# Batches 1 to 7 of x: transposed by DMA from the bf16 copy in SBUF, where TensorE transposed them through PSUM

## The chip, the cores and the metric

The kernel runs on one core of one Trainium2 chip. The metric is the device time of one execution in microseconds; the median of the runs is compared. Durations inside the kernel come from one profiled execution of it.

## The reference

For 8 batches, 8 heads, 512 tokens of x, 32 state rows and a head width of 64, tokens read the state and the state reads the tokens; both results are joined and go through a gated feed-forward layer.

```python
scores = scale * x @ state.T            # per batch and head, softmax over the 32 state rows
xread  = softmax(scores) @ state
scores2 = scale * state @ x.T           # softmax over the 512 tokens
sread  = softmax(scores2) @ x
a = concat([xread, sread])              # (8 * 544, 512): heads side by side
gate = 1 / (1 + exp(-(a @ w_gate)))     # 512 -> 1536
val  = a @ w_val
out  = (gate * val) @ w_out             # 1536 -> 512, float32
```

## The kernel before

**The work of a batch.** Matmul operands are bf16. The token scores need x with the head width on the partitions, so every batch of x is transposed: `at_xT` takes the bf16 copy `xb` (tokens on the partitions, 4 chunks c of 128 tokens, 512 columns each). In two halves, i = 0 and 1, PE makes eight 128x128 transposes into a PSUM tile `xTp` (line 107), and DVE copies the tile to `xT` in SBUF (line 108). `at_S` then multiplies `xT` with the state: half i covers the chunks 2i and 2i+1, with eight matmuls of 64 columns (line 117), and ACT takes the exponential (line 119). `at_norm`, `at_aT` and `at_sr` normalise, transpose the attention weights (`aT`) and compute the state's read.

**The feed-forward part.** `sw_tile` multiplies the state of a batch with the gate and value weights once (`SW`, line 177), so that `gv` makes gate and value rows straight from `aT` and `SW` (line 192, ACT tanh at 199, DVE product at 200). `out_mm` multiplies the result with the output weights (line 209). ACT evicts each finished tile `res` (line 213) and SP stores it (line 216).

**The order.** It is written by hand: a loop over b (the batch in its feed-forward part) and, inside, over f from 0 to 11. One step f holds a third of an output tile of batch b-1, a 128-row piece of gate and value of batch b, one `sw_tile` of batch nb = b+1, and one stage of the attention of batch nb. Each engine works through its instructions in this order. Batch 0's attention runs ahead of the loop. In the steps that matter here:

```python
if f == 0:
    at_xT(nb, 0)
    if b > 0 and nb + 1 < B:
        load_x(nb + 1)
elif f == 1:
    at_xT(nb, 1)
elif f == 2:
    at_S(nb, 0)
elif f == 3:
    at_S(nb, 1)
```

**The queues.** Nearly all transfers are issued by SP, in program order: loads of x (`load_x`, 1 MB), of the weights (`load_w`, `load_wo`), and the stores of `out_mm`, the last of which in an iteration comes at f = 11. GpSimd (POOL) casts each x to bf16 (`cast_x`, line 89) at f = 11 of the iteration before the one that transposes it, behind the casts of `Eb` (line 124); batch 1 is cast ahead of the loop.

Of the kernel before, what the change touches and what calls it, by code (L numbers as in the profile page):

```python
# [9 lines left out]
BF = mybir.dt.bfloat16  # L10
# [6 lines left out]
def kernel(  # L17
# [13 lines left out]
    nc = tc.nc  # L31
# [12 lines left out]
    ap_ = ctx.enter_context(tc.tile_pool(name="ap", bufs=2))  # L44
# [14 lines left out]
    xfs, wfs, xbs, xTs = {}, {}, {}, {}  # L59
# [3 lines left out]
    def load_x(b):  # L63
        xf = stg.tile((128, H, 4, D), FP, name="xf", tag="stg")
        v = x[b].rearrange("h (p c) d -> p h c d", c=4)
        if b == 0:
            for i in range(2):
                nc.sync.dma_start(xf[:, 4 * i:4 * i + 4], v[:, 4 * i:4 * i + 4])
        else:
            nc.sync.dma_start(xf, v)  # L70
        xfs[b] = xf

    def load_w(src, key, q):
        wf = stg.tile((128, 4, 512), FP, name="wf", tag="stg")
        nc.sync.dma_start(wf, src.rearrange("(k p) n -> p k n", p=128)[:, :, q * 512:(q + 1) * 512])
        wfs[key, q] = wf

    def load_wo(q):
        wf = stg.tile((128, 4, 512), FP, name="wof", tag="stg")
        nc.sync.dma_start(wf, moe_w_out.rearrange("(k p) n -> p k n", p=128)[:, 4 * q:4 * q + 4])  # L80
        wfs["o", q] = wf
# [13 lines left out]
    def cast_wo(q):  # L95
        for i in range(4):
            nc.gpsimd.tensor_copy(wo[:, 4 * q + i], wfs["o", q][:, i])


    def at_xT(b, i):  # L100
        if i == 0:
            xTs[b] = ap_.tile((128, 4, 512), BF, name="xT")
        ps = p_at.tile((128, 2, 4, 128), BF, name="xTp", tag="at")
        for jj in range(2):
            for c in range(4):
                j = 2 * i + jj
                nc.tensor.transpose(ps[:, jj, c], xbs[b][:, c, 2 * j:2 * j + 2].rearrange("p h d -> p (h d)"), ident)  # L107
        nc.vector.tensor_copy(xTs[b][:, 2 * i:2 * i + 2], ps.rearrange("p j c t -> p j (c t)"))  # L108

    def at_S(b, i):  # L110
        if i == 0:
            E1s[b] = ap_.tile((128, 4, H * Ns), FP, name="E1")
        ps = p_at.tile((128, 2, H * Ns), FP, name="Sp", tag="at")
        for cc in range(2):
            c = 2 * i + cc
            for j in range(4):
                nc.tensor.matmul(ps[:, cc, j * 64:(j + 1) * 64], xTs[b][:, j, c * 128:(c + 1) * 128],  # L117
                                 sTz[:, b, j, 0:64], start=True, stop=True)
        nc.scalar.activation(E1s[b][:, 2 * i:2 * i + 2], ps, AF.Exp, scale=scale)  # L119

    def at_Eb(b):
        Ebs[b] = ap_.tile((128, 4, H * Ns), BF, name="Eb")
        for c in range(4):
            nc.gpsimd.tensor_copy(Ebs[b][:, c], E1s[b][:, c])  # L124

    def at_norm(b, i):
        if i == 0:
            abs_[b] = ap_.tile((128, 4, H * Ns), BF, name="ab")
        E = E1s[b][:, 2 * i:2 * i + 2].rearrange("p c (h n) -> p (c h) n", n=Ns)
        rs = ap_.tile((128, 16), FP, name="rs")  # L130
        nc.vector.tensor_reduce(rs, E, AX.X, ALU.add)  # L131
        ri = ap_.tile((128, 16), FP, name="ri")
        nc.vector.reciprocal(ri, rs)  # L133
        nc.vector.tensor_tensor(abs_[b][:, 2 * i:2 * i + 2].rearrange("p c (h n) -> p (c h) n", n=Ns), E,  # L134
                                ri.unsqueeze(2).to_broadcast((128, 16, Ns)), ALU.mult)

    def at_aT(b):
        ps = p_at.tile((128, 2, 4, 128), BF, name="aTp", tag="at")
        for g in range(2):
            for c in range(4):  # L140
                nc.tensor.transpose(ps[:, g, c], abs_[b][:, c, g * 128:(g + 1) * 128], ident)  # L141
        aTs[b] = ap_.tile((128, 2, 512), BF, name="aT")
        nc.vector.tensor_copy(aTs[b], ps.rearrange("p g c t -> p g (c t)"))
# [23 lines left out]
    def sw_tile(b, t):  # L167
        if t == 0:
            SWs[b] = fp.tile((128, 2, 2, dff), BF, name="SW", bufs=2)
        q, w, g = t // 4, (t // 2) % 2, t % 2  # L170
        ps = p_sw.tile((128, 512), FP, name="swp")
        W = wg if w == 0 else wv
        for jj in range(2):
            j = 2 * g + jj
            flat = sTz[:, b].rearrange("p j e -> p (j e)")
            lo = j * 128 - 64 * jj
            nc.tensor.matmul(ps, flat[:, lo:lo + 128], W[:, j, q * 512:(q + 1) * 512],  # L177
                             start=(jj == 0), stop=(jj == 1))
        nc.scalar.activation(SWs[b][:, g, w, q * 512:(q + 1) * 512], ps, AF.Copy)  # L179


    def gv(b, f):
        n = 512 if b < B else B * Ns
        if f == 0:
            glus[b] = fp.tile((128, NF, n), BF, name="glu", bufs=2, padded_shape=(128, NF, 512))
        fs = slice(f * 128, (f + 1) * 128)
        pss = []
        for w in range(2):
            ps = p_gv.tile((128, 512), FP, name="gvp", tag="gv")[:, :n]
            if b < B:  # L190
                for g in range(2):
                    nc.tensor.matmul(ps, SWs[b][:, g, w, fs], aTs[b][:, g], start=(g == 0), stop=(g == 1))  # L192
            else:
                for j in range(4):
                    nc.tensor.matmul(ps, (wg if w == 0 else wv)[:, j, fs], XS[:, j], start=(j == 0), stop=(j == 3))  # L195
            pss.append(ps)
        th = fp.tile((128, 512), FP, name="th")[:, :n]

        nc.scalar.activation(th, pss[0], AF.Tanh, scale=0.5)  # L199
        nc.vector.scalar_tensor_tensor(glus[b][:, f], th, 1.0, pss[1], ALU.add, ALU.mult)  # L200
# [3 lines left out]
    def out_mm(b, k):  # L204
        c, f0 = k // 3, (k % 3) * 4
        if f0 == 0:
            ops[b, c] = p_out.tile((128, 512), FP, name="outp")
        for f in range(f0, f0 + 4):
            nc.tensor.matmul(ops[b, c], glus[b][:, f, c * 128:(c + 1) * 128], wo[:, f],  # L209
                             start=(f == 0), stop=(f == NF - 1))  # L210
        if f0 == 8:
            res = fp.tile((128, 512), FP, name="res")
            nc.scalar.activation(res, ops[b, c], AF.Copy, scale=0.5)  # L213
            if b < B:
                rows = out[b * SC:b * SC + S].rearrange("(p c) n -> c p n", c=4)
                nc.sync.dma_start(rows[c], res)
            else:
                for i in range(4):
                    r0 = (4 * c + i) * SC + S
                    nc.sync.dma_start(out[r0:r0 + Ns], res[i * Ns:(i + 1) * Ns])  # L220
# [46 lines left out]
    for b in range(B + 1):  # L267
        for f in range(NF):
            nb = b + 1 if b + 1 < B else None
            if b == 0:  # L270
                if f % 4 == 0:
                    for t in range(f, f + 4):
                        sw_tile(0, t)
                if f == 1:
                    load_w(moe_w_gate, "g", 2)
                    load_w(moe_w_val, "v", 2)
                if f in (4, 5, 6):
                    load_wo(f - 4)
                if f in (8, 9, 10):
                    cast_wo(f - 8)  # L280
            if b > 0:
                out_mm(b - 1, f)
            gv(b, f)
            if nb is not None:
                sw_tile(nb, f)
                if f == 0:
                    at_xT(nb, 0)
                    if b > 0 and nb + 1 < B:
                        load_x(nb + 1)
                elif f == 1:  # L290
                    at_xT(nb, 1)
                elif f == 2:
                    at_S(nb, 0)
                elif f == 3:
                    at_S(nb, 1)
                elif f == 4:
                    at_norm(nb, 0)
                    at_Eb(nb)
                elif f == 5:
                    at_norm(nb, 1)  # L300
                elif f == 6:
                    at_aT(nb)
                elif f == 8:
                    at_sr(nb)
                if b == 0 and f == 9:
                    load_x(2)
                if nb + 1 < B and f == 11:
                    cast_x(nb + 1, nc.gpsimd, range(4))
            if b == 0 and f in (3, 7):
                cast_w(f // 4 + 1)  # L310
# [32 lines left out]
```

## Time and profile before

| | us |
|---|---|
| median of 3 runs | 294.54 (294.14 to 294.59) |
| the profiled execution | 292.45 |
| its span | 290.7 |
| PE matmuls busy, of the span | 254.0 (87%) |
| VectorE (DVE) busy | 131.7 (45%) |
| ScalarE (ACT) busy | 152.8 (53%) |
| GpSimd (POOL) busy | 37.4 (13%) |

The span runs from the first to the last recorded instruction; the profiled execution's time is 1.75 us longer than its span. PE's busy share is an average over a slow start, a long middle in which the loop over f runs, and the end. TensorE's granted clock is full in every slice of the page. The rows name engines as PE (matmul), PEld (weight load, which overlaps PE), DVE, ACT, POOL and SPq (SP's queue of DMA issues).

### The profile page before, as it was taken

The page shows a single profiled execution, that of the slowest core. Times are in us where ns is not written, and L with a number is a line of the kernel's source. Part 1 is how long each engine was busy: PE and PEld are TensorE (multiplying, and loading weights), DVE is VectorE, ACT ScalarE, POOL GpSimd, SP SyncE. Part 2 cuts the span into 40 slices and gives each one's busy share as a digit, 9 for nine tenths or more (in the row PEclk, how much of TensorE's full clock was granted, in tenths as well). Part 3 has the DMA queues.
Part 4 walks back from the last instruction along what each step waited for, and adds up shares of the span by engine and source line. Part 5 has one row for each costly group of instructions (what it writes and reads, how often), then busy time and mean ns, then how long its engine had stood idle before and what let it go on. Part 6 is the DMA issues. An engine that isn't in the chain of part 4 may idle for free.

```text
span 290.7 us, 4172 instructions
## 1 busy us (share of the span) xinstructions
PE 254.0 (87%) x1600; PEld 130.8 (45%) x1600; DVE 131.7 (45%) x216; ACT 152.8 (53%) x264; POOL 37.4 (13%) x78
## 2 busy tenths in 40 slices
PE   0044688599999999999999999999999999999993
PEld 0034243245454545454545454545454544456651
DVE  3026364654554455445544554455445543342210
ACT  0333378675755575557555655565566554432330
POOL 0006016800500050005000500050002000000000
PEclk9999999999999999999999999999999999999999
DMA  7977706900110611061105101511101001011102
GB/s 229 338 241 270 293 2 227 341 12 6 53 41 29 177 54 38 28 178 53 39 26 182 48 37 33 183 39 36 38 36 39 36 36 39 36 72 38 72 37 72
DMA packets 20276, 27.53 MB, mean 95 GB/s; under 512 B 3104, under 2 KB 11296, under 8 KB 20256
## 3 DMA queue, kind: packets, MB, share of 16 engines
q1 hardware_dynamic: 18080, 26.74, 27.1%
q10 hardware_dynamic: 2176, 0.52, 0.9%
q8 instruction: 12, 0.20, 0.3%
q14 instruction: 8, 0.07, 0.1%
HBM read 18.35 MB, written 8.91 MB: 94 GB/s over the span
## 4 chain that ended last, share of the span: by engine, by line
PE 77%; DVE 10%; DMA 5%; ACT 4%; issue 1%; ACTq 0%; DVEq 0%
PE outp L209 28%; PE gvp L192 25%; PE swp L177 12%; DMA sf<-in_state_dram 5%; PE gvp L195 4%; PE xTp L107 3%; DVE glu L200 3%; DVE rs L131 3%; DVE ab L134 2%; PE aTp L141 2%; PE srp L157 1%; PE srp L152 1%; ACT wv L93 1%; PE Sp L117 1%; DVE ri L133 1%
## 5 line engine op out<-in xcount | busy, mean ns | idle before, releaser
L200 DVE SCALAR_TENSOR_TENSOR glu<-th,gvp 128x512 bf16<-128x512 f32 (+1 forms) x108 | 70.9, 657 | 124.4 <-ACT th L199 107.4
L209 PE MATMUL outp<-wo,glu 128*128 128x512 bf16 x408 | 104.1, 379 | 0.7 <-ACT res L213 0.7
L192 PE MATMUL gvp<-aT,SW 128*128 128x512 bf16 x384 | 99.7, 382 | 0.1
L199 ACT ACTIVATE th<-gvp 128x512 f32<-128x512 f32 (+1 forms) x108 | 61.7, 572 | 65.5 <-PE gvp L192 55.1
L179 ACT ACTIVATE SW<-swp 128x512 bf16<-128x512 f32 x96 | 56.9, 597 | 30.3 <-PE swp L177 30.3
L192 PEld LDWEIGHTS <-SW 128*128 128x128 bf16 x384 | 37.5, 98 | 45.6 <-ACT SW L179 1.6
L209 PEld LDWEIGHTS <-glu 128*128 128x128 bf16 x408 | 37.9, 98 | 38.0 <-issue 1.0
L124 POOL CAST Eb<-E 128x256 bf16<-128x256 f32 x32 | 13.0, 435 | 179.8 <-ACT E L119 179.8
L177 PE MATMUL swp<-wg,sTz 128*128 128x512 bf16 x96 | 28.9, 389 | 6.4 <-DVE wg L92 6.4
L177 PEld LDWEIGHTS <-sTz 128*128 128x128 bf16 x192 | 19.0, 100 | 31.2 <-issue 6.9
L213 ACT ACTIVATE res<-outp 128x512 f32<-128x512 f32 x34 | 20.3, 597 | 21.0 <-PE outp L209 21.0
L177 PE MATMUL swp<-wv,sTz 128*128 128x512 bf16 x96 | 29.0, 389 | 0.7 <-ACT SW L179 0.7
L108 DVE COPY xT<-xTp 128x1024 bf16<-128x1024 bf16 x16 | 11.1, 691 | 13.8 <-PE xTp L107 13.7
L89 POOL CAST xb<-xf 128x512 bf16<-128x512 f32 x28 | 16.8, 642 | 0.8 <-DMA xf<-in_x_dram 0.8
L246 PE MATMUL stp<-ident,sb 128*128 128x128 bf16 x8 | 1.2, 306 | 16.4 <-ACT sb L243 16.4
L134 DVE TENSOR_TENSOR ab<-E,ri 128x512 bf16<-128x512 f32 x16 | 12.6, 785 | 0.6
L141 PE MATMUL aTp<-ident,ab 128*128 128x128 bf16 x64 | 6.6, 231 | 5.9 <-DVE ab L134 5.2
L107 PE MATMUL xTp<-ident,xb 128*128 128x128 bf16 x128 | 10.6, 230 | 1.1 <-DVE xb L89 1.1
L131 DVE TENSOR_REDUCE rs<-E 128x16 f32<-128x512 f32 x16 | 10.8, 676 | 1.2 <-ACT E L119 1.2
L107 PEld LDWEIGHTS <-xb 128*128 128x128 bf16 x128 | 9.1, 103 | 4.7 <-DVE xb L89 1.4
L119 ACT ACTIVATE E<-Sp 128x512 f32<-128x512 f32 x16 | 9.4, 592 | 3.1 <-PE Sp L117 3.1
L160 DVE RECIPROCAL r<-srp 128x128 f32<-128x128 f32 x8 | 7.7, 957 | 4.0 <-PE srp L157 4.0
(31 smaller groups left out, 102.6 us busy)
## 6 DMA issues: line engine op xcount, KB each, us to landing
out_dram<-res SPq DMA_DIRECT2D x32, 256.0 KB, 2.2
xf<-in_x_dram SPq DMA_DIRECT2D x7, 1024.0 KB, 7.2
wf<-in_moe_w_gate_dram SPq DMA_DIRECT2D x3, 1024.0 KB, 8.3
wf<-in_moe_w_val_dram SPq DMA_DIRECT2D x3, 1024.0 KB, 5.3
wof<-in_moe_w_out_dram SPq DMA_DIRECT2D x3, 1024.0 KB, 5.0
xf<-in_x_dram SPq DMA_DIRECT2D x2, 512.0 KB, 4.8
sf<-in_state_dram ACTq DMA_DIRECT2D x8, 64.0 KB, 8.0
out_dram<-res SPq DMA_DIRECT2D x8, 64.0 KB, 1.7
```

The lines of the kernel that those rows point to most:

```text
L89: eng.tensor_copy(xb.rearrange("p c h d -> p h c d")[:, 2 * i:2 * i + 2], xf[:, 2 * i:2 * i + 2])
L107: nc.tensor.transpose(ps[:, jj, c], xbs[b][:, c, 2 * j:2 * j + 2].rearrange("p h d -> p (h d)"), ident)
L124: nc.gpsimd.tensor_copy(Ebs[b][:, c], E1s[b][:, c])
L131: nc.vector.tensor_reduce(rs, E, AX.X, ALU.add)
L134: nc.vector.tensor_tensor(abs_[b][:, 2 * i:2 * i + 2].rearrange("p c (h n) -> p (c h) n", n=Ns), E, ri.unsqueeze(2).to_broadcast((128, 16, ...
L177: nc.tensor.matmul(ps, flat[:, lo:lo + 128], W[:, j, q * 512:(q + 1) * 512], start=(jj == 0), stop=(jj == 1))
L179: nc.scalar.activation(SWs[b][:, g, w, q * 512:(q + 1) * 512], ps, AF.Copy)
L192: nc.tensor.matmul(ps, SWs[b][:, g, w, fs], aTs[b][:, g], start=(g == 0), stop=(g == 1))
L199: nc.scalar.activation(th, pss[0], AF.Tanh, scale=0.5)
L200: nc.vector.scalar_tensor_tensor(glus[b][:, f], th, 1.0, pss[1], ALU.add, ALU.mult)
L209: nc.tensor.matmul(ops[b, c], glus[b][:, f, c * 128:(c + 1) * 128], wo[:, f], start=(f == 0), stop=(f == NF - 1))
L213: nc.scalar.activation(res, ops[b, c], AF.Copy, scale=0.5)
```

## The change

The two calls of `at_xT` inside the loop go. In their place, at f = 0, SP issues four DMA transposes per batch, one per chunk of 128 tokens: each reads 128 x 512 bf16 (128 KB) of `xb` and writes 128 x 4 x 128 of `xT`. Batch 0 is still transposed by PE. Everything else is as before.

```diff
+    def at_xT_dma(b):
+        xTs[b] = ap_.tile((128, 4, 512), BF, name="xT")
+        v = xTs[b].rearrange("p j (c t) -> p j c t", c=4)
+        for c in range(4):
+            nc.sync.dma_start_transpose(v[:, :, c], xbs[b][:, c].rearrange("p h d -> p (h d)"))
...
                 if f == 0:
-                    at_xT(nb, 0)
+                    at_xT_dma(nb)
                     if b > 0 and nb + 1 < B:
                         load_x(nb + 1)
-                elif f == 1:
-                    at_xT(nb, 1)
                 elif f == 2:
                     at_S(nb, 0)
```

On SP, at the turn from one iteration to the next, the kernel before has a store, the load of x and the next stores (the words in brackets are what the instruction waits for: a DMA lane's semaphore, or an engine's).

```order
L216 DMA out_dram<-res 128x512 [waits Activation_49]
L70 DMA xf<-in_x_dram 128x8x256 [waits DMAHW3_49,Pool_49]
L216 DMA out_dram<-res 128x512 [waits Activation_49]
L216 DMA out_dram<-res 128x512 [waits DMAHW4_49,Activation_49]
L216 DMA out_dram<-res 128x512 [waits DMAHW5_49,Activation_49]
```

After the change the same place (the store of f = 11 in the iteration of b = 1, then b = 2) reads:

```order
L222 DMA out_dram<-res 128x512 [waits DMAHW1_49,Activation_49]
L114 DMA_TRANSPOSE xT<-xb 128x4x128 [waits DMAHW2_49,PE_49,Pool_49]
L114 DMA_TRANSPOSE xT<-xb 128x4x128 [waits DMAHW3_49]
L114 DMA_TRANSPOSE xT<-xb 128x4x128 [waits DMAHW4_49]
L114 DMA_TRANSPOSE xT<-xb 128x4x128 [waits DMAHW5_49]
L70 DMA xf<-in_x_dram 128x8x256 [waits DMAHW6_49]
L222 DMA out_dram<-res 128x512 [waits DMAHW7_49,Activation_49]
```

The four transposes stand between the store and the load of x; the first of them waits for POOL's cast and for earlier readers of the buffer.

In the first iteration, b = 0, SP has after the change the transposes of batch 1 ahead of the last third of the gate and value weights and of the output weights:

```order
L114 DMA_TRANSPOSE xT<-xb 128x4x128 [waits DMAHW7_49,Pool_49]
L114 DMA_TRANSPOSE xT<-xb 128x4x128 [waits DMAHW0_49]
L114 DMA_TRANSPOSE xT<-xb 128x4x128 [waits DMAHW1_49]
L114 DMA_TRANSPOSE xT<-xb 128x4x128 [waits DMAHW2_49]
L75 DMA wf<-in_moe_w_gate_dram 128x4x512 [waits DMAHW3_49,Activation_49]
L75 DMA wf<-in_moe_w_val_dram 128x4x512 [waits DMAHW4_49]
L80 DMA wof<-in_moe_w_out_dram 128x4x512 [waits DMAHW5_49,DVE_49]
```

Before, the gate weights' load followed the loads of the second third directly.

On PE, `at_S` (lines 117 before, 123 after) waited for DVE's copy of `xT`; now, at f = 2 of the iteration b = 2, it reads as follows.

```order
L183 MATMUL swp<-wv,sTz 128x512
L123 LDWEIGHTS xT [waits DMAHW2_49]
L123 MATMUL Sp<-sTz,xT 128x64 [waits PE_49]
L123 LDWEIGHTS xT
L123 MATMUL Sp<-sTz,xT 128x64
...
L123 LDWEIGHTS xT [waits DMAHW3_49]
L123 MATMUL Sp<-sTz,xT 128x64
```

The first four matmuls wait for the first of the four DMA transposes alone, the next four for the second; the second half of `at_S`, at f = 3, waits in the same way for the third and the fourth.

## Rows read from the trace of the kernel before

**Rows 1.** Busy time by stage: PE, PEld, DVE, ACT, POOL; clock, DMA share, GB/s.
```profile
100.00:130.00 30.00, 29.85 (x190) 14.96 (x189) 14.95 (x24) 18.29 (x32) 3.72 (x8) 1.00 0.23 71
```
**Rows 2.** The chain that ended last, by line, from the page.
```profile
PE outp L209 28%; PE gvp L192 25%; PE swp L177 12%; DMA sf<-in_state_dram 5%; PE gvp L195 4%; PE xTp L107 3%; DVE glu L200 3%; DVE rs L131 3%; DVE ab L134 2%; PE aTp L141 2%; PE srp L157 1%; PE srp L152 1%; ACT wv L93 1%; PE Sp L117 1%; DVE ri L133 1%
```
**Rows 3.** The two costs of the transpose among the page's costliest groups.
```profile
L108 DVE COPY xT<-xTp 128x1024 bf16<-128x1024 bf16 x16 | 11.1, 691 | 13.8 <-PE xTp L107 13.7
...
L107 PE MATMUL xTp<-ident,xb 128*128 128x128 bf16 x128 | 10.6, 230 | 1.1 <-DVE xb L89 1.1
```
**Rows 4.** Timeline of PE, iteration b = 2 (start, us, instruction).
```profile
91.60 1.03 PE L209 MATMUL outp<-wo,glu 128*128 128x512 bf16 x4
...
93.76 1.03 PE L209 MATMUL outp<-wo,glu 128*128 128x512 bf16 x4
...
95.91 0.61 PE L107 MATMUL xTp<-ident,xb 128*128 128x128 bf16 x8
96.36 1.03 PE L209 MATMUL outp<-wo,glu 128*128 128x512 bf16 x4
...
98.97 1.03 PE L209 MATMUL outp<-wo,glu 128*128 128x512 bf16 x4
...
101.12 0.40 PE L117 MATMUL Sp<-sTz,xT 128*128 128x64 bf16 x8
...
103.52 0.40 PE L117 MATMUL Sp<-sTz,xT 128*128 128x64 bf16 x8
```
**Rows 5.** Timeline of PE, iteration b = 0.
```profile
37.22 0.61 PE L107 MATMUL xTp<-ident,xb 128*128 128x128 bf16 x8
37.67 1.03 PE L192 MATMUL gvp<-aT,SW 128*128 128x512 bf16 x4
...
40.70 0.40 PE L117 MATMUL Sp<-sTz,xT 128*128 128x64 bf16 x8
...
42.23 0.40 PE L117 MATMUL Sp<-sTz,xT 128*128 128x64 bf16 x8
```
**Rows 6.** Timeline of SP's queue, iteration b = 2.
```profile
93.28 0.33 SPq L216 DMA_DIRECT2D out_dram<-res  x1
93.71 0.39 SPq L70 DMA_DIRECT2D xf<-in_x_dram  x1
```
**Rows 7.** Page: DMA issues (count, KB each, us from issue to landing).
```profile
out_dram<-res SPq DMA_DIRECT2D x32, 256.0 KB, 2.2
...
wof<-in_moe_w_out_dram SPq DMA_DIRECT2D x3, 1024.0 KB, 5.0
...
sf<-in_state_dram ACTq DMA_DIRECT2D x8, 64.0 KB, 8.0
out_dram<-res SPq DMA_DIRECT2D x8, 64.0 KB, 1.7
```
**Rows 8.** Page: the queue of the state's loads (packets, MB, share of 16 engines).
```profile
q10 hardware_dynamic: 2176, 0.52, 0.9%
```
**Rows 9.** Timeline of POOL.
```profile
24.50 2.74 POOL L89 CAST xb<-xf 128x512 bf16<-128x512 f32 x4
...
44.89 2.28 POOL L97 CAST wo<-wof 128x512 bf16<-128x512 f32 x4
...
55.74 2.65 POOL L89 CAST xb<-xf 128x512 bf16<-128x512 f32 x4 [0.79 <-DMA xf<-in_x_dram]
...
76.61 2.29 POOL L89 CAST xb<-xf 128x512 bf16<-128x512 f32 x4
```
**Rows 10.** Timeline of PE, iteration b = 1.
```profile
72.19 0.40 PE L117 MATMUL Sp<-sTz,xT 128*128 128x64 bf16 x8
...
74.58 0.40 PE L117 MATMUL Sp<-sTz,xT 128*128 128x64 bf16 x8
```
**Rows 11.** Timeline of SP's queue, iteration b = 0.
```profile
27.26 0.37 SPq L75 DMA_DIRECT2D wf<-in_moe_w_val_dram  x1
31.70 14.01 SPq L80 DMA_DIRECT2D wof<-in_moe_w_out_dram  x3
```

## The prediction

> **What bounds the kernel now.** I read the busy time by stage first. In the middle of the run, while the loop over f turns, PE is busy 29.85 of 30.00 us, DVE about 15 and ACT about 18, at the full granted clock [rows 1]. So PE sets the pace there, and DVE and ACT have 40% or more to spare. The chain that ended last agrees: its largest shares are PE's matmuls of lines 209, 192 and 177, and PE's transposes of x (line 107) stand in it with 3% [rows 2]. The timeline of PE shows how these cost. A step f without a transpose takes 93.76 - 91.60 = 2.16 us; a step with one takes 96.36 - 93.76 = 2.60 and 98.97 - 96.36 = 2.61 us [rows 4]. The eight transposes of a half therefore hold PE 0.44 to 0.45 us, whatever the durations of single records say: the mean of 230 ns of one matmul [rows 3] is pipelined and must not be multiplied by eight.
>
> **What is removed.** Each batch has two halves, so 0.89 us of PE. Seven batches lose them (nb = 1 to 7; batch 0 keeps its own), 7 x 0.89 = 6.2 us. That PE can use the time follows from the steps that have no transpose today: they run at 2.16 us with the same ACT and DVE work [rows 4]. The iteration b = 0 is less simple, since PE waits there for casts of weights. But its two transposes lie in a stretch where the next matmul starts at once (37.22 to 37.67, 0.45 us [rows 5]), and what follows, ACT's and DVE's work on these tiles and then the casts, stands behind them in program order; I count it in full, and at worst lose its 0.9. DVE loses 14 copies of 691 ns [rows 3]; it idles half of the time, so I cost that at nothing.
>
> **What is added: four DMA transposes per batch on SP.** The question is whether they land before PE comes to `at_S`, because PE works in order: if `at_S` waits, `gv` and `out_mm` behind it wait too. Two things set the budget, when SP can issue and when PE needs the data.
>
> For b = 2 to 6 (batches 3 to 7) SP comes to the transposes behind the store of f = 11, at 93.28; the load that stands there now goes out at 93.71 [rows 6]. `at_S` starts its first half at 101.12 and its second at 103.52 [rows 4]; less the 0.89 us that PE gains ahead of both, 100.23 and 102.63. Chunk 0 has 6.5 us, chunk 1 a tenth more (four short matmuls), and chunks 2 and 3 have 8.9 us. POOL's cast is long done: for batch 3 it ends at 76.61 + 2.29 = 78.90 [rows 9].
>
> For batch 1 SP waits for the cast, which ends at 24.50 + 2.74 = 27.24 [rows 9]; the halves of `at_S` come at 40.70 and 42.23 [rows 5], less 0.89: 12.6 and 14.1 us. For batch 2 the cast ends at 58.39 [rows 9], and the halves come at 72.19 and 74.58 [rows 10]: 12.9 and 15.3 us. Only five batches are tight.
>
> **What one transpose costs** no row shows. Bounds: a plain store of 256 KB, twice its size, lands 2.2 us after its issue [rows 7] and holds SP 0.33 us [rows 6]. Issued 0.43 us apart, as SP's two issues are, the last would land at 3 x 0.43 + 2.2 = 3.5 us. A transpose surely moves in smaller pieces; the nearest row is the state's loads, whose 2176 packets (0.52 MB, some 240 B each) took 0.9% of 16 engines' span, 42 us, or 19 ns each [rows 8]. By that 128 KB are some 550 packets, 0.65 us on 16 engines: an estimate from those rows. If SP, on the other hand, could not issue one before the last has landed, 4 x 2.2 = 8.8 us against 8.9: it still just fits, and chunk 1 has 4.4 against 6.6. The upper bound of landing is those same state loads, 8.0 us each [rows 7], in the crowd of the start. I take a pace between the two, 1 to 1.5 us from one transpose to the next and 2.2 to land, which puts the last at 5 to 7 us: nearest to the store, since by then the queue holds nothing but the 256 KB store ahead of them. So I cost the wait at nothing. The cover is PE's steps f = 0 to 2, and it is gone when the first lands after 6.5 us or the pace passes 2.2 us.
>
> **What is queued behind them on SP.** In b = 0 the loads of the last weights go out after the transposes. The gate weights wait until about 27.26 + 4 x 1.3 = 32.5, and the output weights' first load, issued at 31.70 now [rows 11], goes at some 33.5; 5.0 us later [rows 7] it is in, at 38.5, and POOL casts it at 44.89 [rows 9], less the gained 0.89: 5 us of cover. In b = 1 SP waits until 58.4 for the cast of batch 2, and the load of batch 3 behind it goes out at about 63.6 and lands by 74; POOL has its cast at 76.61 [rows 9] behind casts of `Eb`, which wait for PE anyway. Later loads of x slip by some 5 us and have most of an iteration. Stores slip too, and nothing waits for them soon: three `res` buffers, one tile every three steps.
>
> **The sum.** 292.45 - 6.2 = 286.2 us for a profiled execution. The median is 2.1 us above the profiled execution, and a shorter PE stream changes nothing in what lies around the span, so I carry the same difference to it: 294.54 - 6.2 = 288.3 us.
>
> **Rivals.**
>
> *The transposes land late, by little.* If each lands as the state's loads did, 8.0 us after issue, chunk 0 comes at 101.71 against 100.23, 1.48 us late, and chunk 1, issued 0.43 us later, another 0.3: 1.8 us per batch, 9.0 us over the five tight batches, less 6.2: 297.3 us, slower. It decides against the change once the stall passes 6.2 / 5 = 1.24 us per batch, a landing of about 7.4 us for the first, or, in a chain, 2.5 us from one to the next. For it: small pieces, a store and then a 1 MB load on the same engines. Against it: the state's loads shared the engines with several megabytes, and here the DMA share is 0.23 [rows 1]. Between 6.5 and 7.4 us part of the gain is left, 289 to 294.
>
> *The crossbar takes block by block.* A batch has 16 blocks of 128x128. If each costs what the smallest transfers cost to land, 1.7 us [rows 7], a batch takes 27.2 us. The five tight batches stall 27.2 - 8.9 = 18.3 us each, batch 1 13.1 and batch 2 11.9, in all 116 us, less 6.2: about 405 us. For it speaks only that no row shows the operation; against it, that SP issues four instructions and not 16, each on all the engines if it is split like others. The Trainium skill, VectorE: DVE Perf Modes, section "The three transpose paths", gives 390 ns on TensorE and 1309 ns by the DMA crossbar for one 128x128 bf16 block, and its rules say to use TensorE where a PSUM destination will do; by 1309 ns a batch would take 20.9 us and the kernel about 361. The trace disagrees with the first figure as a cost to PE (0.45 us for eight), and none of its rows bears on the second; one block timed alone would hold a whole landing, which four transfers in a queue share.
>
> *PE's time is freed but not used.* If ACT or DVE ended the steps f = 0 and 1 instead, the time would stay at 294.5. Rows 1 speak against it, and so does the 2.16 us of the steps beside them.
>
> **How the numbers follow.** Landing in time 0.72 (287.3 to 289.3, allowing for b = 0's 0.9 us and the spread of the runs); late by a part, still a gain, 0.09; freed but unused 0.04; late with a loss of up to some 5 us 0.08; block by block 0.07. A difference of 0.2%, 0.6 us, is about what can be told from none. Faster: 0.72 + 0.09 = 0.81; same 0.04; slower 0.15. The range takes in the first three cases, 287.3 to 294.6, and leaves out 0.15 above.
>
> **What would show it.** Steps f = 0 and 1 at 2.16 us in PE's timeline, 16 transposes of line 107 in place of 128, and no idle time of PE ahead of line 123. The transposes' issues on SP's timeline give the pace, and the DMA table the landing: under 6.5 us for the first and 8.9 us for the last I am right. I am wrong if PE waits ahead of line 123 for a DMA of `xT`: in all of f = 2 and 3, it is the landing or the block rate; only in b = 0, the loads' order on SP. A wait of DVE or POOL for weights in b = 0 would be the slipped loads.

## The result, and the profile after

The median falls from 294.48 to 286.81 us (four executions each, 294.14 to 294.59 and 286.15 to 287.50): a ratio of 0.974, with an interval of 0.971 to 0.977. The direction was forecast; the size was not. The time lies half a microsecond below the range, and the change counts 7.7 us where 6.2 were predicted. The two profiled executions differ by less than that, 292.45 and 287.37 us. This gap, 7.7 between the medians and 5.1 between the traces, is what the experiments had to explain.

The trace after shows the mechanism as forecast. PE's timeline in the iteration b = 2 (start, us, instruction) has no matmul of line 107 any more:

```profile
92.45 1.03 PE L215 MATMUL outp<-wo,glu 128*128 128x512 bf16 x4
...
94.61 1.03 PE L215 MATMUL outp<-wo,glu 128*128 128x512 bf16 x4
...
96.77 1.03 PE L215 MATMUL outp<-wo,glu 128*128 128x512 bf16 x4
...
98.93 0.40 PE L123 MATMUL Sp<-sTz,xT 128*128 128x64 bf16 x8
...
101.32 0.40 PE L123 MATMUL Sp<-sTz,xT 128*128 128x64 bf16 x8
```

The steps f = 0 and 1 take 94.61 - 92.45 = 2.16 and 2.16 us, where they took 2.60 and 2.61 [rows 4]. From the start of f = 0 to `at_S` it is 6.48 us, and was 7.36.

SP's timeline at the same place, and the instructions that touch `xT`, with the landing of the transfers:

```profile
91.98 0.33 SPq L222 DMA_DIRECT2D out_dram<-res  x1
92.42 5.15 SPq L114 DMA_TRANSPOSE xT<-xb  x4
97.61 0.58 SPq L70 DMA_DIRECT2D xf<-in_x_dram  x1
```

```profile
L114 SPq DMA_TRANSPOSE xT<-xb x28: 1195/1258/1595, 27.3 to 208.9; - x28
...
DMA to landing us min/median/max: 2.4/2.5/4.0
```

A transpose holds SP for a median of 1.26 us, and the next goes out 1.3 us after it; the median landing is 2.5 us after the issue. So the last lands at some 92.42 + 3 x 1.3 + 2.5 = 98.8, and PE comes to the second half of `at_S` at 101.32: 2.5 us to spare, and 4 us for the first. The list of what PE waited for (engine and line, for whom, us in total, times, longest) has no DMA of `xT`:

```profile
PE stp L252 <- ACT sb L249: 16.4, 2, 12.4
PE swp L183 <- DVE wg L92: 6.4, 3, 2.9
PE aTp L147 <- DVE ab L140: 6.1, 6, 2.0
PE xTp L107 <- DVE xb L89: 1.1, 1, 1.1
PE outp L215 <- ACT res L219: 0.7, 1, 0.7
PE Sp L123 <- DVE xT L108: 0.7, 1, 0.7
PE swp L183 <- ACT SW L185: 0.7, 2, 0.4
```

The one wait of `Sp` is batch 0's, on DVE, as before. In the middle of the run PE is as full as it was [rows 1]; DVE is busy 14.25 us and was 14.95, and the share of the DMA engines is 0.37 and was 0.23:

```profile
100.00:130.00 30.00, 29.86 (x185) 14.57 (x184) 14.25 (x23) 18.51 (x33) 4.98 (x10) 1.00 0.37 109
```

### The profile page after: what moved, and what is told of

Read it like the earlier page. It is cut to its first block, busy times and chain, and to the rows that moved or that the text cites. A ratio compares the mean times of both kernels' runs of the same rounds, so it can differ in the third digit from the quotient of the medians.

```text
span 285.3 us, 3976 instructions
## 1 busy us (share of the span) xinstructions
PE 248.2 (87%) x1488; PEld 124.6 (44%) x1488; DVE 122.6 (43%) x202; ACT 152.6 (53%) x264; POOL 39.1 (14%) x78
## 3 DMA queue, kind: packets, MB, share of 16 engines
q1 hardware_dynamic: 33312, 30.42, 34.8%
## 4 chain that ended last, share of the span: by engine, by line
PE 76%; DVE 11%; DMA 5%; ACT 4%; issue 2%; ACTq 0%; DVEq 0%
PE outp L215 28%; PE gvp L198 25%; PE swp L183 12%; DMA sf<-in_state_dram 5%; PE gvp L201 4%; DVE rs L137 3%; DVE glu L206 3%; DVE ab L140 3%; PE aTp L147 2%; PE srp L163 1%; PE srp L158 1%; ACT wv L93 1%; DVE ri L139 1%; PE Sp L123 1%; ACT th L205 1%
## 5 line engine op out<-in xcount | busy, mean ns | idle before, releaser
L89 POOL CAST xb<-xf 128x512 bf16<-128x512 f32 x28 | 18.2, 692 | 2.6 <-PE swp L183 1.8
L147 PEld LDWEIGHTS <-ab 128*128 128x128 bf16 x64 | 4.4, 102 | 9.6 <-DVE ab L140 7.9
L123 PEld LDWEIGHTS <-xT 128*128 128x128 bf16 x128 | 6.2, 102 | 4.1 <-DVE xT L108 0.8
L252 PEld LDWEIGHTS <-sb 128*128 128x128 bf16 x8 | 0.7, 131 | 16.7 <-ACT sb L249 16.7
```

What stands on the lines that cost most here:

```text
L89: eng.tensor_copy(xb.rearrange("p c h d -> p h c d")[:, 2 * i:2 * i + 2], xf[:, 2 * i:2 * i + 2])
```

## The experiments

Each was compared with executions of the kernel before on the same chip. The chip is another one in each of three groups (the runs up to batch 1 by PE, the next four, the last four), so differences between groups hold less firmly than those within one. Two theories stood against each other on the missing 1.5 us: A, that the kernel before is in most executions some 2 us longer than the profiled one, for a reason inside the span; and B, that a fixed 2 us lies around the span, and the change won 7.7 us inside it.

### The kernel before, and the one after, again

No edit. Expected of the kernel before:

> The kernel before, unchanged. Theory A (the profiled execution before, 292.45 us, was a lucky one, and most executions carry some 2 us more that is no fixed part around the span): spans vary from about 290.7 to 293 us, and the longer ones show a lower mean granted clock. Theory B (a fixed 2 us lies around the span in runs that are not profiled, and the change gained 7.7 us inside the span): every execution has a span of 290.7 us within 0.5, at the same clock.

Expected of the changed one:

> The changed kernel, unchanged. Theory A: its spans lie at 284.2 to 285.6 us, some with a clock of 0.994 to 0.997 and some at 1.0, and the ratio to the kernel before depends on which executions are met: between 0.973 and 0.983. Theory B: ratio 0.974 each time.

Medians: 292.55 us (12 executions, 292.02 to 294.35) and 287.47 us (6, 287.33 to 288.52); other executions of the kernel before in the same comparison, 17, have a median of 294.24 (292.15 to 295.24). So the same kernel against itself has a ratio of 0.996 with an interval of 0.993 to 0.999, which leaves out 1: groups of executions differ by more than such an interval allows for. The changed kernel's ratio is 0.979 here (0.975 to 0.982), within the 0.973 to 0.983 of theory A, where the first comparison gave 0.974. The span of the kernel before, too, varies, 290.2 to 293.4 us, and the time is always 1.7 to 1.9 us more than the span (1.9 to 2.1 us in the changed kernel). That ends B. The 2 us lie inside the span, and the mean granted clock goes with them. Over the 51 executions of the kernel before that three comparisons gave (12 + 17 here, and 11 + 11 below), and the ten of the changed kernel so far:

| mean clock | before: executions, median us | after: executions, median us |
|---|---|---|
| 0.996 and above | 22, 292.55 | 3, 286.25 |
| 0.990 to 0.995 | 13, 293.61 | 7, 287.50 |
| below 0.990 | 16, 294.81 | none |

The rows overlap a little in time: the second goes up to 294.57, the third starts at 294.18. The clocks of the executions of the first comparison, 294.14 to 294.59, are not on record. But of the 51 no execution at 0.996 or above took more than 293.07 us, and the 19 that took 294.14 or more have 0.984 to 0.994. So those four were, as far as this goes, executions with a lowered clock. At equal clock the change is worth 6.3 and 6.1 us.

### No transposes at all

Leaves out the transposes of batches 1 to 7; their scores use batch 0's transposed x.

```diff
-            xTs[b] = ap_.tile((128, 4, 512), BF, name="xT")
+            xTs[b] = wp.tile((128, 4, 512), BF, name="xT0")
...
-                    at_xT_dma(nb)
+                    xTs[nb] = xTs[0]
```

> Leaves out the transposes of batches 1 to 7 altogether: their scores are computed with batch 0's transposed x. If the DMA transposes are hidden fully, the time is that of the changed kernel within 0.3% (some 286.8 us). If they cost something anywhere (contention of transfers, SP held for 5 us per batch, DVE or POOL slowed), it is faster than the changed kernel by that much, 1 us or more.

287.23 us (6 executions, 286.04 to 287.91), against 287.47 and 286.81 for the changed kernel; the shortest are 286.04 and 286.15. In these times the 28 DMA transposes cost nothing that can be told from the spread. The traces show a small cost. In the changed kernel's first trace PE waits for DVE's normalised weights `ab` in six places, 6.1 us in all, where the kernel before had three; the new ones stand in the batches 4, 5 and 6. That of batch 5, and the list of the kernel before:

```profile
164.89 0.51 PE L147 MATMUL aTp<-ident,ab 128*128 128x128 bf16 x6 [0.34 <-DVE ab L140]
```

```profile
PE aTp L141 <- DVE ab L134: 5.2, 3, 2.0
```

From one batch's `at_aT` to the next it is 28.94 us before and 28.04 or 28.05 without transposes, each time; the changed kernel has 28.04 once and then 28.20, 28.24 and 28.16 (from 108.03 to 220.67): 0.5 us lost. The kernel without transposes has three waits for `ab`, 5.1 us.

What changed ahead of `ab` is the load of x. It goes out behind the transposes, at 154.21 here; with its median landing of 6.2 us it is in at 160.4. POOL's cast of that x started right behind POOL's earlier work, and now starts with the landing. Before, then after:

```profile
163.43 2.29 POOL L89 CAST xb<-xf 128x512 bf16<-128x512 f32 x4
```

```profile
160.36 2.74 POOL L89 CAST xb<-xf 128x512 bf16<-128x512 f32 x4 [0.70 <-PE swp L183]
```

In the three batches with waits the first `ab` takes DVE 1.01 to 1.10 us, where it takes 0.90 without transposes, and the cast runs beside it. That the later cast makes it longer is not shown: in other batches it runs beside an `ab` of 0.90 or less.

### Batch 1 by PE

```diff
-                    at_xT_dma(nb)
+                    if nb == 1:
+                        at_xT(nb, 0)
+                    else:
+                        at_xT_dma(nb)
...
+                elif f == 1 and nb == 1:
+                    at_xT(nb, 1)
```

> Batch 1 is transposed by PE as before, batches 2 to 7 by DMA. The forecast counted 0.89 us for batch 1. The trace after shows 0.46 us by the first matmul behind the cast of the second weight slice (44.39 before, 43.93 after), because ACT and not PE ends that stretch. If that reading is right, this kernel's trace has that matmul at 44.4 us, and its span is 0.4 to 0.5 us longer than the changed kernel's at equal clock; if batch 1 was worth 0.89, it is 0.9 us longer.

288.49 us (6, 287.76 to 289.45), 1.0 us over the changed kernel on the same chip. The matmul came at 45.17, not at 44.4, since the first weight matmul itself starts at 31.6 to 32.2 us in different executions. From there to the matmul behind the second cast it is 12.98 us here, 12.26 to 12.96 in five traces of the kernel before, and 11.77 to 12.19 in the three without PE's transposes of batch 1 (the changed kernel twice, and no transposes at all).

That spread comes from PE's rate. From the first weight matmul on, four matmuls of 512 columns take 33.42 - 31.72 = 1.70 us, where four take 0.86 in the middle of the run. The rate doubles at about 36.8 us, not at the same moment in every execution. The clock column of the views reads 1.00 there all the same. In the first pair of traces (before, then after):

```profile
36.79 0.60 PE L177 MATMUL swp<-wg,sTz 128*128 128x512 bf16 x2
...
44.39 1.04 PE L177 MATMUL swp<-wg,sTz 128*128 128x512 bf16 x4 [1.76 <-DVE wg L92]
```

```profile
36.81 1.01 PE L183 MATMUL swp<-wg,sTz 128*128 128x512 bf16 x2
37.65 1.03 PE L198 MATMUL gvp<-aT,SW 128*128 128x512 bf16 x4
...
43.93 1.04 PE L183 MATMUL swp<-wg,sTz 128*128 128x512 bf16 x4 [1.76 <-DVE wg L92]
```

The two matmuls at 36.8 hold PE 37.22 - 36.79 = 0.43 us before [rows 5] and 37.65 - 36.81 = 0.84 after: in that execution of the changed kernel the full rate came later, and this hid 0.4 us of the gain. Behind that place all traces agree. From the matmul of `gv` at f = 1 (37.67 and 37.65) to the one behind the second cast it is 6.72 or 6.73 us in the six traces with PE's transposes of batch 1, and 6.28 in four without (the fourth is that of the attention weights by DMA, below); and the first half holds PE 0.45 us in all six. So batch 1 is worth 0.45 + 0.44 = 0.89 us, as the forecast counted it. The reading that ACT ends the stretch was wrong.

### PE kept busy where it waits

21 matmuls that nobody reads fill PE's waits in and ahead of the iteration b = 0. The same edit was made to the kernel before and to the changed one.

```diff
+    def busy(b, n):
+        ps = p_at.tile((128, 512), FP, name="idle", tag="at")
+        for i in range(n):
+            nc.tensor.matmul(ps, ident, xbs[b][:, i % 4].rearrange("p h d -> p (h d)"), start=True, stop=True)
...
     at_sr(0)
+    busy(0, 7)
...
+                    if b == 0:
+                        busy(1, 4)
                     at_aT(nb)
...
             if b == 0 and f in (3, 7):
+                busy(1, 5)
```

> The kernel before with 21 matmuls more on PE whose results nobody reads, put where PE waits in the iteration b = 0 and just ahead of it (7 behind batch 0's attention, 5 ahead of each of the last two weight slices, 4 ahead of batch 1's transposes of the attention weights). Theory A (the 2 us by which many executions of the kernel before are longer are TensorE at its lower clock in and around b = 0, after waits): the spread shrinks, no execution has a mean clock below 0.992, and the median falls to 290 us or below, since the matmuls from 31.7 us on also start nearer to the full rate. Theory B (the 2 us have nothing to do with PE's clock): spread and median stay, 292 to 295 us.

> The same 21 matmuls in the changed kernel. Theory A: the difference to the kept-busy kernel before is what the change itself is worth, 5.4 to 6.0 us, and 7.7 is not met again; the median is 282 to 285 us. Theory B: the difference stays at 7 us or more.

The kernel before: 290.78 us, six executions within 290.68 and 291.01, all at a mean clock of 0.995 or more; the executions without the edit that ran beside it had 292.47 to 295.18. The changed kernel: 285.05 us, 284.62 to 285.85. More work makes the kernel before shorter, and its spread falls from 2.7 us to 0.3; the changed kernel is shorter than in its ten executions without the edit, which ran on other chips. That is theory A; only the medians were expected a little lower, at 290 or below and at 282 to 285. The difference between the two, 5.7 us, is what the change is worth with little of PE's clock in it. By the spans it is 6.05 us (medians 289.0 and 282.95).

The edit does more than keep the clock of the later stretch. The first weight matmuls (before, then before with the edit) no longer run at the lower rate:

```profile
31.72 1.87 PE L177 MATMUL swp<-wg,sTz 128*128 128x512 bf16 x4 [2.93 <-DVE wg L92]
```

```profile
31.73 1.25 PE L182 MATMUL swp<-wg,sTz 128*128 128x512 bf16 x4
```

From there to batch 1's first transpose it is 37.22 - 31.72 = 5.50 us and 35.66 - 31.73 = 3.93: 1.6 us less. That is why the edited kernel is also shorter than the shortest execution beside it, 292.47 us at a mean clock of 0.998.

### Each batch transposed twice

```diff
+        w = ap_.tile((128, 4, 512), BF, name="xTw").rearrange("p j (c t) -> p j c t", c=4)
+        for c in range(4):
+            nc.sync.dma_start_transpose(w[:, :, c], xbs[b][:, c].rearrange("p h d -> p (h d)"))
         for c in range(4):
             nc.sync.dma_start_transpose(v[:, :, c], xbs[b][:, c].rearrange("p h d -> p (h d)"))
```

> Each batch is transposed twice by DMA, first into a buffer that nobody reads. At 1.29 us from one transpose to the next and 2.5 us to land, the needed ones land at 7.7, 8.9, 10.2 and 11.5 us after SP comes to them, against budgets of 6.5, 6.6, 8.9 and 9.0: if PE waits as the forecast's rival says, a stall of some 2.2 us in each of the five batches 3 to 7, 11 us in all, some 298 us. If something else than the budget hides the transposes, the time stays near 287 us.

305.87 us (4, 304.83 to 308.18), 8 us more than expected. Now PE waits, in the way of the forecast's first rival; PE's timeline in the iteration b = 2, and its longest waits:

```profile
100.67 0.29 PE L126 MATMUL Sp<-sTz,xT 128*128 128x64 bf16 x4 [1.05 <-DMA xT<-xb]
101.96 0.29 PE L126 MATMUL Sp<-sTz,xT 128*128 128x64 bf16 x4 [0.99 <-DMA xT<-xb]
```

```profile
PE stp L255 <- ACT sb L252: 16.8, 2, 13.2
PE Sp L126 <- DMA xT<-xb: 13.3, 12, 1.9
```

The first two chunks cost 2.0 us here and 2.0 to 2.5 in the other tight batches, as expected; ten such waits, and two more at the second half of `at_S`, make 13.3 us. The span is longer by 17.7 (303.0 and 285.3), and the clock may account for most of the rest. It is lowered in stretches that stand at 1.00 in the changed kernel's first trace: one in the iteration b = 0, and one behind PE's longest wait for a first half.

```profile
56.00:62.00 6.00, 5.94 (x40) 2.69 (x40) 1.31 (x2) 3.77 (x7) 4.38 (x8) 0.72 0.28 94
160.00:168.00 8.00, 5.47 (x27) 2.29 (x26) 1.38 (x2) 3.47 (x6) 0.74 (x2) 0.83 0.52 105
168.00:176.00 8.00, 7.95 (x42) 3.67 (x42) 4.71 (x8) 5.00 (x9) 3.31 (x6) 0.95 0.62 197
```

6 x 0.28 + 8 x 0.17 + 8 x 0.05 = 3.4 us, at most, since PE also idles in the second stretch. Some 1 us or more stays open, and so does the wait at the second halves, which the expectation did not have.

### The attention weights by DMA as well

```diff
+    def at_aT_dma(b):
+        aTs[b] = ap_.tile((128, 2, 512), BF, name="aT")
+        v = aTs[b].rearrange("p g (c t) -> p g c t", c=4)
+        for c in range(4):
+            nc.sync.dma_start_transpose(v[:, :, c], abs_[b][:, c])
...
-                    at_aT(nb)
+                    at_aT_dma(nb)
```

> The same change made once more, for the attention weights: the eight PE transposes of batches 1 to 7 (0.77 us of PE in a batch) and their DVE copy go, and four DMA transposes of 64 KB each make aT. They can go out once DVE has normalised the weights (f = 5) and must land by the next f = 0, some 13 us later. If freed PE time counts in full as it did for x, 7 x 0.77 = 5.4 us less, some 281 to 282 us. Rival: SP now waits for DVE in mid-iteration with stores and the next transposes of x behind it, and PE waits for x again: slower than 287.

283.42 us (6, 281.08 to 284.18), 4.0 us under the changed kernel of the second experiment. The shortest fits the forecast, at a clock of 0.998; the others, 283.12 us and more, have 0.983 to 0.993 and do not. PE's timeline shows a longer wait ahead of the last weight slice, 3.2 us where it was 1.7, since PE has nothing to transpose there:

```profile
54.55 1.04 PE L189 MATMUL swp<-wg,sTz 128*128 128x512 bf16 x4 [3.19 <-DVE wg L92]
```

So part of this gain is probably given back as lower clock; this trace is of the shortest execution and shows none. It has no wait for `aT` or `xT`.

### Both, with PE kept busy

The edit of the attention weights with `busy` at the start (7), at f = 3 (5) and at f = 7 (10).

> The changed kernel with the attention weights transposed by DMA as well, and with 22 matmuls whose results nobody reads where PE waits in and ahead of the iteration b = 0. If the two gains add (5 us of PE time from the attention weights, 2 us and more of lower clock from the kept-busy PE), some 279 us with a spread under 1 us. If the kept-busy part does nothing here, 281 to 284 as without it.

279.65 us (6, 279.18 to 279.88), a ratio of 0.952 to the kernel before, 0.948 to 0.956. Some 279 us were expected. The gains add: 5.4 us under the kept-busy changed kernel, which is 7 x 0.77. This is the fastest version found.

### Three more executions of the kernel before

No edit, for traces at different clocks.

> The kernel before, looked at again for a trace of an execution of 294 us or more. Theory A: the surplus over 292.45 lies between 55 and 70 us of the span, where the granted clock is below 1 for some slices, and the matmuls of 512 columns there follow each other at 0.43 us and not 0.22. If the execution is a short one, 292 to 293 us, no such slice.

> As the run before it: a second look for an execution of 294 us or more.

> As the run before it: a third look for an execution of 294 us or more.

They gave 295.00, 293.55 and 292.66 us, at mean clocks of 0.988, 0.994 and 0.997: one of each row of the table. Busy time by stage (PE, PEld, DVE, ACT, POOL; then the granted clock) of the longest:

```profile
53.00:56.00 3.00, 1.96 (x11) 0.90 (x12) 2.51 (x5) 0.60 (x1) 2.36 (x5) 0.81 1.10 363
56.00:58.00 2.00, 0.86 (x3) 0.28 (x3) 1.33 (x2) 1.71 (x2) 1.22 (x3) 0.50 1.04 337
58.00:60.00 2.00, 2.00 (x5) 0.55 (x4) 0.00 (x0) 1.77 (x3) 1.47 (x3) 0.50 0.52 170
60.00:62.00 2.00, 2.00 (x7) 0.76 (x6) 0.00 (x0) 1.28 (x3) 0.00 (x0) 0.58 0.00 0
```

And of the shortest:

```profile
53.00:56.00 3.00, 1.70 (x11) 0.79 (x12) 2.63 (x4) 1.81 (x3) 2.23 (x5) 1.00 1.05 334
56.00:58.00 2.00, 1.31 (x6) 0.56 (x7) 0.38 (x1) 2.00 (x3) 2.00 (x4) 1.00 1.02 336
58.00:60.00 2.00, 1.96 (x10) 0.69 (x9) 0.00 (x1) 1.74 (x4) 0.53 (x1) 1.00 0.15 52
60.00:62.00 2.00, 2.00 (x31) 1.41 (x30) 1.41 (x2) 0.90 (x2) 0.00 (x0) 1.00 0.03 8
```

The clock column is 0.50 from 56 to 60 us in the one, the lower of TensorE's two levels, and 1.00 in the other. PE's timelines of the same stretch, the longest first:

```profile
57.39 1.89 PE L177 MATMUL swp<-wg,sTz 128*128 128x512 bf16 x4 [1.14 <-DVE wg L92]
59.22 1.86 PE L177 MATMUL swp<-wv,sTz 128*128 128x512 bf16 x4
60.88 1.42 PE L192 MATMUL gvp<-aT,SW 128*128 128x512 bf16 x4
```

```profile
56.44 1.04 PE L177 MATMUL swp<-wg,sTz 128*128 128x512 bf16 x4 [1.69 <-DVE wg L92]
57.73 1.08 PE L177 MATMUL swp<-wv,sTz 128*128 128x512 bf16 x4 [0.25 <-ACT SW L179]
58.65 1.24 PE L192 MATMUL gvp<-aT,SW 128*128 128x512 bf16 x4
```

The same four matmuls take 1.89 us and 1.04. The spans differ by 2.4 us (293.2 and 290.8). The execution in between has a clock of 0.72 at 56 to 58, 0.50 at 58 to 60 and 0.92 at 60 to 62, and a span of 291.7. Most of the 2.4 us lies here, a little earlier than expected (53 to 62, not 55 to 70): from the third weight slice's first matmul to the next pair of weight matmuls behind `gv` it is 62.14 - 57.39 = 4.75 us and 59.73 - 56.44 = 3.29, 1.5 us more. Another 0.7 us comes earlier, from the moment at which the rate doubles behind 31.7 us (from the first weight matmul to the one behind the second cast 12.94 and 12.26 us), and 0.3 us between the second slice and the third.

## Why the prediction was right and wrong

**The step that failed** is this one: "The median is 2.1 us above the profiled execution, and a shorter PE stream changes nothing in what lies around the span, so I carry the same difference to it". The difference did not lie around the span, where the kernel before has 1.7 to 1.9 us in every execution. The profiled execution had a mean clock of 0.998; the three timed ones, by their times, had less. In such executions PE runs at its lower level for some microseconds around 53 to 62 us, after its waits in the iteration b = 0: the table, the three traces and the matmuls that fill these waits show it for the kernel before. The ten executions of the changed kernel had less of it (mean clocks of 0.992 to 1.0; the trace of one at 0.994 has 0.61 from 57 to 60 us), so the median fell by the change's own gain, some 6 us, and by most of that surplus. The gain against equal clocks is 6.3 and 6.1 us; with PE kept busy it is 5.7. By 292.45 - 6.2, the sum for an execution with little of this, 286.2 us were forecast; the changed kernel's three executions at 0.996 and above have 286.15, 286.25 and 287.37. Whether the changed kernel is less prone to the low clock is not settled: none of ten executions fell below 0.990, of the kernel before 16 of 51 did, and 3 of 6 with the attention weights moved as well.

**PE's time removed.** 0.44 to 0.45 us a half, 0.89 us a batch: right, by the timeline (7.36 to 6.48 us). The sum of 6.2 us for seven batches holds within the spread. The first pair of traces shows 5.3 us by `at_S` of batch 7 (216.88 and 211.57): 0.4 us less by the later full rate in the iteration b = 0, and 0.5 by the waits for `ab`. So the third rival, time that is freed and not used, came true for 0.5 us of 6.2, in another step than it named. What lies around the span is not quite the same either, some 0.2 us more after the change; why stays open.

**Batch 1** was counted in full, and gave it: 0.89 us at equal rates, 1.0 us by the medians, with spreads as large. The 0.46 us of the first pair is 0.89 less the 0.4 by which the full rate came later.

**One transpose's cost.** The pace was taken as 1 to 1.5 us and the landing as 2.2 us; 1.3 and 2.5 were measured. Packets were estimated at some 550 a transpose; by SP's queue, before and after (packets, MB, share of 16 engines), they are (33312 - 18080) / 28 = 544:

```profile
q1 hardware_dynamic: 18080, 26.74, 27.1%
```

```profile
q1 hardware_dynamic: 33312, 30.42, 34.8%
```

The pace goes with SP's issue, 1.26 of the 1.3 us, rather than with the engines: if the other transfers took as long as before, the two shares make 0.73 us on 16 engines for a transpose (0.65 estimated).

**The cover** was right in size for the first half: when a second set stands in front, PE waits there 2.0 to 2.5 us in each tight batch, where 2.2 us follow from the budgets. The first rival itself did not come.

**The block-by-block rival** did not come. The Trainium skill, VectorE: DVE Perf Modes, section "The three transpose paths", has 1309 ns for one block by the crossbar. Here 1.3 us passed from one instruction of four blocks to the next, so the trace does not agree with that as a price for each block.

**What is queued behind them.** The loads of weights slipped at no cost: PE's waits for weights are 6.4 us after, and before:

```profile
PE swp L177 <- DVE wg L92: 6.4, 3, 2.9
```

That later loads of x "have most of an iteration" was wrong. Before, a load that went out at 151.55, with a median landing of 7.2 us, was cast at 163.43: 4.7 us of cover, less than the 5.2 us that four transposes take. The cast now starts when the load is in, and the waits for `ab` appear with it.

## What to carry to other kernels

A transpose on a full PE can be moved to the DMA crossbar if the data is known early enough: count SP's 1.3 us per instruction and 2.5 us to land against the time until PE comes to the reader, queue and all, and count the cover of every load that slips behind them. Before carrying a gap between a profiled execution and a median from one kernel to another, look at where it lies: if time minus span is constant from execution to execution, the gap is inside, and the granted clock by stage is the first thing to compare. Look at the spacing of equal matmuls as well: the column read 1.00 where they ran at half their rate. PE's waits for weights can cost twice, once as waits and once as clock; 21 matmuls that nobody reads brought 2.8 us here against the executions beside them, and a spread of 0.3.

## What was not expected of the hardware

**A transpose's price on SP hardly depends on its size.** The four transposes of `xT`, 128 KB each, hold SP 1.26 us each; those of `aT`, 64 KB each, 1.23 us:

```profile
L155 SPq DMA_TRANSPOSE aT<-ab x28: 1179/1230/2096, 49.6 to 217.7; - x28
```

**Two stretches of PE that look alike may be followed by different clocks.** From 51 to 55 us PE was busy 2.05 of 4.00 us in the execution whose clock fell to 0.50 at 55 us and 2.00 in the one whose clock stayed at 1.00. What decides it is not settled.

**Filling waits helped more than leaving PE idle.** With 21 matmuls more the kernel before became 2.8 us shorter at the median (290.78 against 293.61 beside it), and its shortest execution 1.8 us (290.68 against 292.47 beside it; 292.02 is the shortest of all 51). Of this, 1.6 us come from the first weight matmuls, which the clock column shows at 1.00 in both.
